# Attention of the first two batches as quads of heads in 64x64 tiles, and the first MLP product of batch 0 in 64x64 tiles at two banks

## The chip, the cores and the metric

The kernel runs on one core of one Trainium2 chip. The metric is the device time of one execution in microseconds. The core has a matrix engine (TensorE, PE in the profile; its weight loads are PEld), VectorE (DVE), ScalarE (ACT), GpSimd (POOL) and SyncE (SP). Each engine takes its own instructions in the order written and waits on semaphores for the others. Matmuls read SBUF and write PSUM, which has eight banks of 128 x 512 float32.

## The reference

Attention with a softmax whose denominator has one more term, then an MLP with a squared ReLU. Batch is 8, heads 12, sequence 448, head size 64; 3584 tokens, model width 768, hidden width 2048.

```python
scores = scale * np.matmul(q, k.transpose(0, 1, 3, 2))
m = np.max(scores, axis=-1, keepdims=True)
e = np.exp(scores - m)
attn = e / (np.sum(e, axis=-1, keepdims=True) + np.exp(-m) + 1e-09)
x = np.matmul(attn, v)
h = x @ w_in
out = (np.maximum(h, 0.0) ** 2) @ w_out
```

Inputs and output are float32; the kernel computes in float16 with float32 sums.

## The kernel before

**Order.** The schedule is written by hand: program order is each engine's order. Every batch passes three stages: scores, exp, sums and values (attention, into `xt`); first MLP product with squared ReLU (into the ring `gs`); second MLP product (into `ot`, then stored). The attention of one batch is interleaved with the MLP of the batch before it, in lists of visits with shares of MLP work between them.

**Batches 2 to 7** take heads in quads: four heads at once, keys in chunks of 64, all products in 64x64 tiles, so that four small products run side by side. `visit` (L317) computes one chunk's scores of four heads into a pair of banks `sp` and its exp; `add_quad` (L350) adds the chunks on DVE; `sums_quad` (L365) multiplies by ones on TensorE and takes the reciprocal with Ln and Exp on ACT; `values_quad` (L381) multiplies with V and normalises. Batch 2's transposes are made by TensorE (`transposes_quad`, L184), later ones by the DMA queue from staged copies.

**Batches 0 and 1** take heads in pairs with keys in chunks of 112 (four neighbouring tokens to a partition). `scores` (L228) has products of 64x112, `values` (L269) of 112x64, `transposes` (L207) of 112x64. Each array shape is another mode of TensorE. `add_chunks` (L247) adds the exps on DVE, `row_sums` (L277) sums over partitions on TensorE and takes the reciprocal, `normalise` (L294) multiplies. Batch 0 is done in two query ranges, of 192 and 256, so that the MLP of the first can run while the second is computed. 18 units (pair, range) follow each other in three loops; `drain` puts pieces of the first MLP product of batch 0 between their steps by shares that were fixed by hand. `keep_warm` (L590) puts filler matmuls between the first transposes.

**MLP.** `product` (L415) runs either as two products of 128x64 or whole. `tile_in` (L435) makes 128 hidden columns for up to 512 tokens in one bank from `mp_tile` (L404), `relu_squared` (L425) evicts it with one ReLU (DVE, or ACT for some) and one square on DVE; `tiles_in_early` (L450) starts before the last heads are there. `tile_out` (L477) makes the second product.

**PSUM.** `sp`: two pairs of banks, for scores. `mp`: three single banks, `xp`: one; from the end of batch 1 `mp_tile` takes turns among the four.

**Loads.** q and k of the first three pairs come as float32 over the SP and ACT queues, all else over POOL's queue, converted to float16: V and the remaining pairs of batch 0, `win` in eight parts, batch 1, then two quads of batch 2 and `wout`. POOL's queue keeps the written order.

Of the kernel before, what the change touches and what calls it, by code (L numbers as in the profile page):

```python
# [16 lines left out]
def kernel(  # L17
# [14 lines left out]
    NPAIR = H // 2  # L32
# [3 lines left out]
    P = S // RUN  # L36
    NQ = H // 4
    KC = S // 64
    PAIRED = (0, 1)
    ON_PE = (0, 1, 2)  # L40
    COLS = H * S // 2 + 16
    HALF = DM // 2

# [19 lines left out]
    m_psum = ctx.enter_context(tc.tile_pool(name="m_psum", bufs=3, space=bass.MemoryType.PSUM))  # L63
# [9 lines left out]
    q_r = q.rearrange("b h (p t) d -> b p h t d", t=RUN)  # L73
    k_r = k.rearrange("b h (p t) d -> b p h t d", t=RUN)
    v_r = v.rearrange("b h (p t) d -> b p h t d", t=RUN)
    win_r = moe_w_in.rearrange("(c p) f -> p c f", p=128)
    wout_r = moe_w_out.rearrange("(c p) f -> p c f", p=128)

    whole, vns, qks, xts, naturals, stages = {}, {}, {}, {}, {}, {}

    def quads_of(t, t0, n, run):

        return t[:, :, t0:t0 + n * run].rearrange("b (i x) (p t) d -> b i p x (t d)", i=2, t=run)

    def load_v_quads(b):
        vn = vns[b] = v_pool.tile([128, NQ, 2, KC, D], FP16, name="vn")
        for i in range(2):
            rows_ = vn[64 * i:64 * i + 64].rearrange("p g j c d -> p (g j) (c d)")
            parts = ((0, KC),) if b in ON_PE else ((0, KC - 1), (KC - 1, KC))
            for c0, c1 in parts:  # L90
                nc.gpsimd.dma_start(out=rows_[:, :, c0 * D:c1 * D], in_=quads_of(v, 64 * c0, 64, c1 - c0)[b, i])

    def load_natural_quads(b, g0, g1):
        t = nat.tile([128, RUN * 2 * S], FP16, name=f"nn{0 if g0 == 0 else 1}")
        w = 2 * S
        for n, r in enumerate((q, k)):
            part = t[:, n * (g1 - g0) * w:(n + 1) * (g1 - g0) * w].rearrange("p (h x) -> p h x", x=S)
            for i in range(2):
                nc.gpsimd.dma_start(out=part[64 * i:64 * i + 64], in_=quads_of(r, 0, 64, KC)[b, i][:, 2 * g0:2 * g1])
            for g in range(g0, g1):  # L100
                naturals["qk"[n], b, "quad", g] = part[:, 2 * (g - g0):2 * (g - g0) + 2].rearrange(
                    "p j (c d) -> p j c d", d=D)

    def load_v(b, p0, p1):
        hs = slice(2 * p0, 2 * p1)
        if b not in vns:
            vns[b] = v_pool.tile([P, H, RUN, D], FP16, name="vn")
        nc.gpsimd.dma_start(out=vns[b][:, hs], in_=v_r[b, :, hs])

    def load_natural(b, p0, p1):  # L110

        raw = b == 0 and p1 <= 3
        for n, r in (("q", q_r), ("k", k_r)):
            src = r[b, :, 2 * p0:2 * p1]
            if raw:
                if p0 == 0:
                    whole[n] = e_pool.tile([P, RUN * S], FP32, name="et")
                t = whole[n][:, p0 * 512:(p0 + 1) * 512].rearrange("p (h t d) -> p h t d", h=2, t=RUN)
                (nc.sync if n == "q" else nc.scalar).dma_start(out=t, in_=src)
            else:  # L120
                if p0 % 3 == 0 and n == "q":
                    whole["both"] = nat.tile([P, RUN * 2 * S], FP16, name=f"nn{p0 // 3}")
                w = NPAIR * RUN * D
                t = whole["both"][:, w * (n == "k"):w * (n == "k") + w].rearrange("p (h t d) -> p h t d", t=RUN, d=D)
                t = t[:, 2 * (p0 % 3):2 * (p0 % 3 + p1 - p0)]
                nc.gpsimd.dma_start(out=t, in_=src)
            for pr in range(p0, p1):
                naturals[n, b, pr] = t[:, 2 * (pr - p0):2 * (pr - p0) + 2]

    def load_win(i, n):  # L130
        w = DF // n
        nc.gpsimd.dma_start(out=win[:, :, i * w:(i + 1) * w], in_=win_r[:, :, i * w:(i + 1) * w])
# [4 lines left out]

# [30 lines left out]

# [13 lines left out]
    def transposes_quad(b, g):  # L184
        if b not in qks:
            qks[b] = qk_pool.tile([128, 3, COLS], FP16, name="qk")
        for n in range(2):
            tp = mp_tile(FP16).rearrange("p a x -> p (a x)")
            for c in range(KC):
                for j in range(2):  # L190
                    nc.tensor.transpose(tp[64 * j:64 * j + 64, 128 * c:128 * c + 128],
                                        naturals["qk"[n], b, "quad", g][:, j, c, :], ident)
            nc.vector.tensor_copy(  # L193
                qks[b][:, n, 2 * S * g:2 * S * (g + 1)].rearrange("p (i c x) -> p c i x", i=2, c=KC),
                tp[:, 0:2 * S].rearrange("p (c i x) -> p c i x", c=KC, i=2))

    def cast(b, pr):
        for name in "qk":
            f = flat.tile([P, 2, RUN, D], FP16, name=f"flat{name}")
            if pr < 2 and name == "k":  # L200
                nc.scalar.activation(out=f, in_=naturals[name, b, pr], func=AF.Copy)
            else:
                nc.vector.tensor_copy(f, naturals[name, b, pr])
            naturals[name, b, pr] = f

    def transposes(b, pr):
        tp = mp_tile(FP16)  # L207
        for i, name in enumerate("qk"):
            for s in range(RUN):
                for h in range(2):  # L210
                    nc.tensor.transpose(tp[64 * h:64 * h + 64, i, P * s:P * s + P],  # L211
                                        naturals[name, b, pr][:, h, s, :], ident[0:P, 0:P])
        if b not in qks:
            qks[b] = qk_pool.tile([128, 3, COLS], FP16, name="qk")
        parts = (0, S // 2, S) if b == 0 and pr < 3 else (0, S)
        for x, y in zip(parts, parts[1:]):
            nc.vector.tensor_copy(qks[b][:, 0:2, pr * S + x:pr * S + y], tp[:, :, x:y])


# [4 lines left out]
    def chunk(et, u, c, kk):  # L224

        n = u[3]
        if n < S:
            return et[:, 0:RUN * 2 * n].rearrange("p (c h j n) -> p c h j n", c=2, h=2, j=2)[:, c, :, kk % 2, :]  # L228
        return et.rearrange("p (k x) -> p k x", k=RUN)[:, kk]

    def scores(u, et, c, only=(0, 1)):
        b, pr, q0, n = u
        qk = qks[b]
        two = [] if n == S else s_psum.tile([P, 2, 512], FP32, name="sp")
        for kk in [2 * c + x for x in only]:
            sp = s_psum.tile([P, 2, 512], FP32, name="sp") if n == S else two
            o = 0 if n == S else kk % 2 * n
            for h in range(2):
                r = slice(64 * h, 64 * h + 64)
                x = pr * S  # L240
                nc.tensor.matmul(sp[:, h, o:o + n], qk[r, 1, x + P * kk:x + P * kk + P],  # L241
                                 qk[r, 0, x + q0:x + q0 + n], start=True, stop=True)
            if n == S:
                exp(chunk(et, u, c, kk).rearrange("p (o x) -> p o x", o=2), sp[:, :, 0:S])
        if n < S:
            exp(et[:, 0:RUN * 2 * n].rearrange("p (c h x) -> p c h x", c=2, h=2)[:, c], two[:, :, 0:2 * n])

    def add_chunks(u, et, es, half, step):
        n = u[3]
        if n == S:  # L250
            e = et.rearrange("p (k x) -> p k x", k=RUN)
            if step < 2:
                nc.vector.tensor_add((es, half[:, 0:2 * S])[step], e[:, 2 * step], e[:, 2 * step + 1])
            else:
                nc.vector.tensor_add(es, es, half[:, 0:2 * S])
        elif step == 1:
            nc.vector.tensor_add(half[:, 0:4 * n], et[:, 0:4 * n], et[:, 4 * n:8 * n])
        elif step == 2:
            f = half[:, 0:4 * n].rearrange("p (h j n) -> p h j n", h=2, j=2)
            nc.vector.tensor_add(es[:, 0:2 * n].rearrange("p (h n) -> p h n", h=2), f[:, :, 0, :], f[:, :, 1, :])  # L260

    def of_head(e, u, h):

        b, _, _, n = u
        if n < S:
            return e[:, h]
        return e.rearrange("p (h x) -> p h x", h=2)[:, h]

    def values(u, et, xp, o=0):  # L269
        b, pr, _, n = u  # L270
        for kk in range(RUN):
            for h in range(2):
                nc.tensor.matmul(xp[64 * h:64 * h + 64, o:o + n], vns[b][:, 2 * pr + h, kk, :],  # L273
                                 of_head(chunk(et, u, kk // 2, kk), u, h), start=(kk == 0), stop=(kk == RUN - 1))

    def row_sums(us, sums):

        n = us[0][3]
        m = n * len(us)
        zp = mp_tile()  # L280
# [573 lines left out]
```

## Time and profile before

| what | us |
|---|---|
| median of 3 runs (lowest to highest) | 407.35 (407.05 to 407.85) |
| span of the profiled execution | 405.9 |
| PE busy, tails of matmuls included | 394.9 (97%) |
| DVE busy | 277.2 (68%) |
| ACT busy | 224.1 (55%) |
| POOL busy | 59.5 (15%) |
| first exp of batch 0 | 7.54 |
| first scores of batch 1 | 36.21 |
| first visit of batch 2 | 68.59 |
| second MLP tile of batch 1 | 83.06 |

A line of the timeline gives start and duration in us, engine, source line, operation, output<-input, the array shape used (64*112 is 64 rows by 112 columns), the operand's partitions x elements, and how many instructions are merged into it; brackets tell how long the engine was idle before and who released it. A row of the stretches gives the stretch, its length, busy us (instructions) of PE, PEld, DVE, ACT, POOL, granted clock of TensorE, DMA share, and GB/s. The waits give engine, tile and line, whom it waited for, total us, times, longest. Matmuls overlap, and their recorded duration holds a tail: the next starts before it ends.

### The profile page before, as it was taken

How to read it: one execution, taken by the hardware profiler on the slowest of the kernel's cores; microseconds unless marked ns; L12 is line 12 of the kernel's file. 1: busy time of each engine (PE TensorE's matmuls, PEld its weight loads, DVE VectorE, ACT ScalarE, POOL GpSimd, SP SyncE). 2: the span in 40 equal slices, each digit the busy share in tenths (PEclk: the TensorE clock that was granted, in tenths of full speed). 3: DMA queues.
4: the chain of work that ended last, by engine and by line, in shares of the span. 5: the costliest groups of instructions: out<-in, count | busy, mean ns of one | idle time of the engine just before them, and what ended most of it. 6: DMA issues, size and time to landing. Idle time of an engine off the chain costs nothing.

```text
span 405.9 us, 14479 instructions
## 1 busy us (share of the span) xinstructions
PE 394.9 (97%) x6627; PEld 262.4 (65%) x6627; DVE 277.2 (68%) x507; ACT 224.1 (55%) x277; POOL 59.5 (15%) x93
## 2 busy tenths in 40 slices
PE   7899998999999999999999999999999999999997
PEld 3567676667676666757666675757666675555664
DVE  3778888786967867686967867686967868186000
ACT  4898986928465564836466473836466473100111
POOL 6524140005000320003200440005000000000000
PEclk9999999999999999999999999999999999999999
DMA  9999999498706794186925694186501020100222
GB/s 186 197 197 198 203 204 208 105 196 113 175 3 126 122 186 102 42 134 144 189 69 129 119 191 95 42 155 122 120 3 40 3 80 4 48 31 0 79 78 79
DMA packets 77118, 45.83 MB, mean 113 GB/s; under 512 B 46720, under 2 KB 71552, under 8 KB 77056
## 3 DMA queue, kind: packets, MB, share of 16 engines
q0 software_dynamic: 30128, 22.16, 36.5%
q1 hardware_dynamic: 46208, 22.05, 24.5%
q8 instruction: 52, 0.85, 0.9%
q10 hardware_dynamic: 720, 0.69, 0.7%
q14 instruction: 10, 0.08, 0.1%
HBM read 45.69 MB, written 17.93 MB: 157 GB/s over the span
## 4 chain that ended last, share of the span: by engine, by line
PE 87%; DVE 5%; ACT 3%; DMA 2%; issue 1%; ACTq 0%; DVEq 0%
PE mp L491 26%; PE mp L419 22%; PE mp L421 10%; PE xp L419 6%; PE mp L390 6%; PE sp L346 5%; PE xp L421 4%; ACT et L222 2%; DMA et<-in_k_dram 2%; PE sp L241 2%; PE xp L273 2%; PE sp L332 1%; PE mp L211 1%; PE xp L491 1%; PE sp L375 1%
## 5 line engine op out<-in xcount | busy, mean ns | idle before, releaser
L222 ACT ACTIVATE et<-sp 128x896 f16<-128x896 f32 (+3 forms) x132 | 118.0, 915 | 26.0 <-PE sp L346 13.0
L491 PE MATMUL mp<-wout,gs 64*64 64x384 f16 x1760 | 125.6, 323 | 0.0
L419 PEld LDWEIGHTS <-win 128*64 128x64 f16 x1536 | 85.0, 110 | 47.7 <-issue 7.2
L419 PE MATMUL mp<-xt,win 128*64 128x448 f16 (+2 forms) x1248 | 109.0, 324 | 2.2 <-DVE qk L193 1.3
L491 PEld LDWEIGHTS <-gs 64*64 64x64 f16 x2624 | 76.2, 107 | 23.0 <-issue 0.6
L491 PE MATMUL xp<-wout,gs 64*64 64x384 f16 x864 | 84.7, 323 | 0.0
L431 DVE TENSOR_SCALAR rt<-mp 128x448 f16<-128x448 f32 (+2 forms) x82 | 51.0, 622 | 19.0 <-PE mp L419 8.4
L433 DVE TENSOR_TENSOR gs<-rt 128x448 f16<-128x448 f16 (+2 forms) x128 | 50.4, 395 | 12.0 <-ACT rt L429 7.9
L222 ACT ACTIVATE nn<-sp 128x896 f16<-128x896 f32 x42 | 37.6, 913 | 14.0 <-PE sp L346 12.3
L429 ACT ACTIVATE rt<-mp 128x448 f16<-128x448 f32 x18 | 9.8, 543 | 60.0 <-PE mp L419 48.3
L498 DVE TENSOR_SCALAR ot<-mp 128x384 f32<-128x384 f32 x41 | 22.7, 554 | 27.3 <-PE xp L491 19.9
L181 POOL COPY flatq<-qk 64x384 f16<-64x384 f16 x20 | 13.6, 704 | 186.9 <-DMA qk<-stage_k 186.6
L421 PEld LDWEIGHTS <-gs 128*128 128x128 f16 x256 | 24.4, 98 | 15.1 <-issue 0.4
L346 PE MATMUL sp<-qk 64*64 64x224 f16 x720 | 32.9, 258 | 0.0
L419 PE MATMUL xp<-xt,win 128*64 128x448 f16 x288 | 31.3, 352 | 0.0
L421 PE MATMUL mp<-wout,gs 128*128 128x384 f16 (+2 forms) x192 | 29.6, 313 | 0.0
L346 PEld LDWEIGHTS <-qk 64*64 64x64 f16 x720 | 22.4, 119 | 10.7 <-issue 3.6
L500 ACT ACTIVATE ot<-mp 128x384 f32<-128x384 f32 (+2 forms) x12 | 5.6, 463 | 42.4 <-PE mp L421 42.4
L396 DVE TENSOR_TENSOR xt<-mp,rcp 128x448 f16<-128x448 f32 x34 | 19.7, 619 | 8.2 <-PE mp L390 7.8
L378 ACT ACTIVATE rcp<-sp,one_b 128x896 f32<-128x896 f32 x18 | 18.1, 1003 | 6.3 <-PE sp L371 6.3
L390 PEld LDWEIGHTS <-vn 64*64 64x64 f16 x504 | 14.4, 107 | 6.1 <-issue 0.4
L390 PE MATMUL mp<-et,vn 64*64 64x448 f16 x308 | 18.3, 349 | 0.0
(82 smaller groups left out, 392.6 us busy)
## 6 DMA issues: line engine op xcount, KB each, us to landing
out_dram<-ot SPq DMA_DIRECT2D x9, 384.0 KB, 2.3
win<-in_moe_w_in_dram POOLq DMA_DIRECT2D x8, 384.0 KB, 14.0
wout<-in_moe_w_out_dram POOLq DMA_DIRECT2D x4, 768.0 KB, 17.8
vn<-in_v_dram POOLq DMA_DIRECT2D x10, 288.0 KB, 5.4
out_dram<-ot SPq DMA_DIRECT2D x15, 192.0 KB, 3.0
stage_q<-in_q_dram POOLq DMA_DIRECT2D x4, 676.0 KB, 9.8
stage_k<-in_k_dram POOLq DMA_DIRECT2D x4, 676.0 KB, 12.3
out_dram<-ot SPq DMA_DIRECT2D x7, 288.0 KB, 6.0
```

The costliest lines, as they stand in the source:

```text
L181: nc.gpsimd.tensor_copy(km[rows_].rearrange("p h (x o) -> p h x o", o=2)[:, :, :, odd], src[:, :, S // 2 - 32:S // 2])
L222: nc.scalar.activation(out=out_, in_=in_, func=AF.Exp, scale=scale)
L346: nc.tensor.matmul(sp[64 * i:64 * i + 64, o, j * n:(j + 1) * n], keys, qk[r, 0, h * n:(h + 1) * n], start=True, stop=True)
L378: nc.scalar.activation(out=rcp, in_=zp[:, :, 0:S], func=AF.Ln, bias=one_b)
L390: nc.tensor.matmul(xps[i][64 * j:64 * j + 64, 0:S], vns[b][r, g, j, c, :], of_column(e[r], m, j), start=(c == 0), stop=(c == KC - 1))
L396: nc.vector.tensor_mul(xts[b][:, NQ * i + g, :], xps[i][:, 0:S], zqs[m][:, i, :])
L419: nc.tensor.matmul(out_[x:x + 64], lhsT[:, x:x + 64], rhs, start=start, stop=stop)
L421: nc.tensor.matmul(out_, lhsT, rhs, start=start, stop=stop)
L431: nc.vector.tensor_scalar(out=rt[:, 0:m], in0=hp[:, 0:m], scalar1=0.0, scalar2=None, op0=ALU.max)
L433: nc.vector.tensor_mul(gs[:, f0:f0 + per, t0 % RING:t0 % RING + n], r, r)
L491: nc.tensor.matmul(o[y:y + 64, 0:w], g[x:x + 64, y:y + 64], wout[x:x + 64, fb, n0:n0 + w], start=(fb == 0), stop=(fb == NFFB - 1))
L498: nc.vector.tensor_scalar(out=ot[:, n0:n0 + w], in0=op[:, 0:w], scalar1=OUT_SCALE, scalar2=None, op0=ALU.mult)
```

## The change

Batches 0 and 1 use quads too. The pairs' code goes (`scores`, `values`, `transposes`, `add_chunks`, `row_sums`, `normalise`, the three loops, `drain`, `tiles_in_early`, the fillers after the first nine). Batch 1 becomes quads with `visit`, whole query range. Batch 0 becomes quads in two query halves of 224; its sums are made by TensorE, by multiplying every exp chunk with ones beside the values. Its first MLP product is made by `Square` in blocks of 512 hidden columns by 224 tokens: 96 products of 64x64 in a pair of banks, the upper rows writing one bank while the lower rows write the other, then the other way round. Between the two turns a SyncE no-op that waits for the first and releases the second keeps them apart. One ReLU and one square evict 896 columns at once.

Heads are paired anew (heads 2g, 2g+1, 6+2g, 7+2g are a quad), with `win`'s rows laid out to match, in all batches. `mp` and `xp` become one pair of banks each; `mp_pair` and `mp_tile` take turns among the pairs. The two values' banks of a quad are normalised by one multiply instead of two. q and k of the first quad come as float32, in two halves; `win` comes in four parts of two loads each; loads are by quad. The values and the sums of batch 1's last quad fall into batch 2's first visits, where before those of its last pair did.

Core of the new code (all matmuls go through `mm`):

```diff
+    def half_scores(at):
+        g, half, k = HALVES[at]
...
+        for x in range(len(two[0])):
+            for o in range(2):
+                if x < len(two[o]):
+                    c, j = two[o][x]
+                    r = slice(64 * j, 64 * j + 64)
+                    for i in range(2):
+                        s0 = (2 * g + i) * S
+                        mm(sp[64 * i:64 * i + 64, o, x * FIRST:(x + 1) * FIRST], qk[r, 1, s0 + 64 * c:s0 + 64 * c + 64],
+                           qk[r, 0, s0 + q0:s0 + q0 + FIRST], start=True, stop=True)
...
+    def half_post(at):
...
+        if (g, half) not in xzs:
+            xzs[g, half] = pair_of("xp")
+        xz, e = xzs[g, half], half_e(g, half)
+        todo = [p for x in zip(*pieces(at)) for p in x]
+        for is_sum in range(2):
+            for c, j in todo:
+                for i in range(2):
+                    r = slice(64 * i, 64 * i + 64)
+                    key = (g, half, i, j)
+                    mm(xz[64 * j:64 * j + 64, i, is_sum * FIRST:(is_sum + 1) * FIRST],
+                       ones[r] if is_sum else vns[0][r, j, g, c, :], e[r, j, c], start=key not in opened,
+                       stop=bool(is_sum) and c == KC - 1)
...
+    def half_finish(g, half):
...
+        nc.scalar.activation(out=rcp, in_=xz[:, :, FIRST:2 * FIRST], func=AF.Ln, bias=one_b)
+        nc.scalar.activation(out=rcp, in_=rcp, func=AF.Exp, scale=-1.0)
...
+        nc.vector.tensor_mul(xts[0][:, 2 * g:2 * g + 2, q0:q0 + FIRST], xz[:, :, 0:FIRST], rcp)
...
+    def posts(*ats):
+        for at in ats:
+            half_post(at)
+            if HALVES[at][2] == 3:
+                half_finish(*HALVES[at][0:2])
...
+    class Square:
...
+        def part(self, flip, dcs=range(DCH)):
...
+            for jf in range(2):
                 for dc in dcs:
+                    self.done += 1
+                    for o in range(2):
+                        r = (o + flip) % 2
+                        rows_ = slice(64 * r, 64 * r + 64)
+                        for y in (0, 64):
+                            f = (self.f0 + 2 * o + jf) * 128 + y
+                            got = mm(hp[y:y + 64, o, jf * n:(jf + 1) * n], win[rows_, dc, f:f + 64],
+                                     xt[rows_, dc, x0:x0 + n], start=self.done == 1, stop=self.done == total,
+                                     bank=(self.t0, self.f0, o, y), row=r)
+                            if self.last:
+                                after(got, self.last)
+                                self.last = None
+            if self.done < total:
+                self.last = nc.sync.nop()
+                after(self.last, got)
+            if self.done == total:
+                relu_squared(hp[:, :, 0:2 * n], self.t0, n, self.f0, 4, self.act)
...
+    in0 = [Square(0, 4 * x) for x in range(4)]
+    in1 = [Square(FIRST, 4 * x) for x in range(4)]
+    early, late = range(2 * NQ - 2), range(2 * NQ - 2, 2 * NQ)
+    pre = {
+        12: [lambda: in0[0].part(0, early)],
+        15: [lambda: in0[0].part(0, late)],
+        16: [lambda: in0[1].part(0)],
+        17: [lambda: in0[1].part(1)],
+        19: [lambda: in0[2].part(0)],
+        20: [lambda: in0[2].part(1)],
+        22: [lambda: transposes_quad(1, 0, "mp")],
+    }
+    behind = {
+        3: [lambda: transposes_quad(0, 1, "mp")],
+        7: [lambda: transposes_quad(0, 2, "mp")],
+        12: [lambda: in0[0].part(1, early)],
+        14: [lambda: in0[0].part(1, late)],
+    }
+    done = {at: (at - 2,) for at in range(2, 24)}
+    done[12], done[13] = (10, 11), ()
+    for at in range(24):
+        if at > 1:
+            half_scores(at)
+        for f in pre.get(at, ()):
+            f()
+        posts(*done.get(at, ()))
+        if at > 1:
+            half_exp(at)
+        for f in behind.get(at, ()):
+            f()
...
+    plan = {
+        0: [lambda: posts(22)],
+        1: [lambda: in0[3].part(0), lambda: posts(23)],
+        2: [lambda: in0[3].part(1)],
+        3: [lambda: transposes_quad(1, 1, "mp")],
+        5: [lambda: in1[0].part(0)],
+        6: [lambda: in1[0].part(1)],
+        8: [lambda: in1[1].part(0)],
+        9: [lambda: in1[1].part(1), lambda: sums_quad(0, False), lambda: values_of(0, 2)],
+        10: [lambda: values_of(0, 5)],
+        11: [lambda: transposes_quad(1, 2, "mp")],
+        13: [lambda: in1[2].part(0)],
+        14: [lambda: in1[2].part(1)],
+        16: [lambda: in1[3].part(0), lambda: sums_quad(1, False), lambda: values_of(1, 2)],
+        17: [lambda: in1[3].part(1), lambda: values_of(1, 5)],
+        19: [lambda: transposes_quad(2, 0, "mp")],
+        20: [lambda: transposes_quad(2, 1, "xp")],
+    }
```

`HALVES` counts the 24 steps of batch 0: half 0 of quads 0, 1, 2, then half 1, four steps each; `after(a, b)` makes a wait for b. `FIRST` is 224. In `pre` work stands behind a step's scores and ahead of the posts of the step two before; `behind` stands after the step's exp. A group is the four steps of a quad and half, 0 to 3, 4 to 7 and so on; the fourth has one chunk instead of two.

## The prediction

> **What bounds the kernel now.** I read the page first (span, chain), then the busy time by stretch, the waits of the opening, and the timeline at the joints. The run itself is 405.9 us of span; the median of the runs shown is 407.35, so 1.45 us lie around it, and I add them at the end.
>
> ```profile
> span 405.9 us, 14479 instructions
> ...
> PE 87%; DVE 5%; ACT 3%; DMA 2%; issue 1%; ACTq 0%; DVEq 0%
> ```
>
> The chain that ended last is TensorE for 87%. From batch 2 on there is little else: a batch takes 46 us there (its first MLP tile starts at 126.1, 172.3, 218.1 in the chain), and the change alters neither number, shape nor order of its matmuls. What it rebuilds lies before the first visit of batch 2, at 68.59. The stretches (us of busy time of PE, PEld, DVE, ACT, POOL; clock; DMA):
>
> ```profile
> 5.40:36.20 30.80, 28.03 (x476) 19.43 (x476) 22.57 (x50) 26.59 (x36) 12.61 (x17) 1.00 1.43 201
> 36.20:68.60 32.40, 30.16 (x481) 22.04 (x479) 27.75 (x53) 27.38 (x37) 9.52 (x14) 1.00 1.31 204
> 68.60:82.00 13.40, 12.75 (x285) 8.73 (x285) 9.41 (x15) 12.49 (x15) 0.00 (x0) 1.00 0.62 132
> ```
>
> In the opening 63.2 us no engine is full: ACT 54.0, DVE 50.3. PE's 58.2 holds the tails of matmuls, so I count its stream by start distances:
>
> ```profile
> 54.51 1.37 PE L419 MATMUL mp<-xt,win 128*64 128x256 f16 x22
> ...
> 55.80 0.58 PE L241 MATMUL sp<-qk 64*112 64x448 f16 x4
> ...
> 56.24 1.72 ACT L222 ACTIVATE et<-sp 112x896 f16<-112x896 f32 x2
> ...
> 56.32 0.97 PE L191 MATMUL mp<-ident,nn 128*64 128x128 f16 x28
> ```
>
> Eleven pairs of 256 columns at 0.109 make 1.20; the next shape starts after 1.29: a change of array shape costs 0.09. The two exps take 1.72 where one takes 0.92: the next may start after 0.80. Batches 0 and 1 alternate three shapes: I count 72 changes up to 68.6. In batch 2 and later all is 64x64:
>
> ```profile
> 121.52 0.36 PE L346 MATMUL sp<-qk 64*64 64x224 f16 x8
> 121.71 0.97 PE L491 MATMUL mp<-wout,gs 64*64 64x384 f16 x17
> ```
>
> Eight 64x64 products of 224 columns hold the array for 0.19, 24 ns each. Who waited for whom from 5.4 to 68.6:
>
> ```profile
> ACT et L222 <- PE sp L241: 6.4, 11, 2.2
> DVE rt L431 <- PE mp L419: 4.4, 4, 1.4
> ```
>
> **The loads, edit by edit.** TensorE before: MLP 192 pairs (0.0825 and 0.109) 18.4, scores 9.1, values 8.4, sums 2.1, transposes 6.3, warm-up fillers 1.3 = 45.6, and 72 changes at 0.093 = 6.7: 52.3. After, at 24 ns per 224 columns: 8 MLP blocks of 96, 18.4; scores of batch 0 4.4 and of batch 1 4.0; values and sums of batch 0 4.0 each and 0.8 because the first two steps use one half of the rows; values of two quads 2.65, two sums 0.4; transposes 7.3 (seven quads' 28 in 0.82 by L191, and 28 of the first quad at 0.056, as they fill one half of the columns): 46.0, and 20 changes, 1.9: **47.9**. So the quads give back in switching what TensorE pays for the sums.
> ACT before: 24 exps at 0.80, 12 at 0.91, 12 at 0.70, 11 Ln/Exp pairs 13.4, casts 1.3 = 53. After: 39 at 0.81, 6 at 0.43 (L429, 448 elements, 0.54 less the overlap), 6 Ln/Exp at 1.24, 2 at 1.95 (L378, L379), casts 1.2: **46.7**. DVE loses all adds of batch 0 (12.1 by L257, L260): about **42** of 50.3.
> By loads alone all fall. What decides is how long TensorE, which takes its work in written order, stands idle: now 63.2-52.3 = 10.9.
>
> **The new waits, walked.** Every engine keeps the written order. Prices: an exp may start 0.40 after its scores start (0.44 at 68.59/69.03) and blocks the scores two steps on, as `sp` has two buffers; posts (values and sums of a step) 0.38; a quad's transposes 0.82, and its scores can start 1.75 after they began (last matmul's tail 0.22, copy 0.62, hand-overs); half an MLP block 1.15. Not in the trace: ReLU of 128x896, between 0.62 (L431 at 448) and 1.25 (two of them); 384, 448 and 512 elements take 0.552, 0.622, 0.686, so 1.09, and the one `mp` pair is free 1.4 after the block's last matmul. One `xp` pair holds values and sums of a group: the next group's posts can start only after Ln 0.64, Exp 0.58 and the multiply 0.62, so 1.95 after Ln.
>
> ```
>  7.5  exp 0, as now (7.54): same 224 KB, same casts
> 14.3  scores 4: first copies end 10.5 (exp 2 at 10.95), posts 0, 1 at 0.77
>       each, quad 1's transposes 12.5; ACT idle 12.3-14.7
> 20.2  scores 8: quad 2's transposes 18.45; ACT idle 18.7-20.6
> 26.1  Ln of group 2: behind an MLP piece and two posts; ACT idle 1.5
> 34.9  Ln of group 3: late MLP piece ends 30.1 (one turn at the banks shows,
>       0.4), ReLU frees mp 31.5, block half to 32.65, posts 33.05, scores,
>       block half 34.4, posts 34.6; ACT idle 31.7-34.9
> 37.1  posts 16 wait for its multiply; TensorE idle 34.8-37.1
> 41.6  Ln of group 4; posts 20 wait to 43.55 (idle 1.05)
> 44.7  first visit of batch 1 (now 36.2)
> 50.1  transposes: Ln 47.1, multiply 49.0, ReLU 50.1; idle 48.4-50.1
> 55.9  third block: ReLU behind two adds; idle 54.85-55.9
> 66.7  last block: ReLU 65.55-66.65; idle 1.05
> 73.4  first visit of batch 2 (now 68.59)
> ```
>
> Batch 0's 37 us hold some 24 of TensorE work; batch 1's 28.7 hold 23, about what it takes now (32.4 with more MLP in it). TensorE idle 68.0-47.9 = 20.1, **+4.8** at the joint.
>
> Then batch 2's first visits: 48 steps of second product 7.8, 12 scores 2.3, two sums 0.4, and now the values of a whole quad 1.3 = 11.8; the sum of quad 2 waits 0.75 for its last add (last exp ends 73.7, add 0.65), Ln/Exp 1.95 delays the exps and the third to fifth visits wait 0.85: end 86.85, transposes 87.8, second MLP tile 89.0. Now:
>
> ```profile
> 81.60 1.65 PE L419 MATMUL mp<-xt,win 128*64 128x448 f16 x12 [0.64 <-ACT rcp L290]
> 83.06 1.33 PE L419 MATMUL xp<-xt,win 128*64 128x448 f16 x12
> ```
>
> 89.0-83.06 = **+5.9**, of it 1.1 here: the wait for the last pair's reciprocal (0.64 and more inside the 1.65) goes, the longer Ln/Exp comes.
>
> Costed at nothing, with cover. Transfers: at 198 GB/s the first quarter of `win` is in by 20 (used from 24.5), batch 1's quads by 30, 39 and 42 (used 41.6, 50.1, 60.4); batch 2's loads and `wout` now start behind the transposes at 42.5 and end by 63, used after 75; were it not so, a 4 us piece would show. PSUM in pairs of banks from batch 2 on: a pair waits for two evictions, but ReLU and square take 1.02 (L431, L433) against 1.13 of a tile, and the multiply of a quad comes once: between -0.3 and +0.5 in all, I take 0. Turns through SyncE: ten; nine have 0.57 or more of other work before the next piece. The nearest row for SyncE is its 0.4 per issue, so each could show 0 to 0.4: 0 to +3.6, I take 0.4, as SP has nothing else queued there.
>
> The clock: 1.00 in all stretches above, with fillers between the first transposes. The change drops those. [...] No row here shows a halved clock.
> [...]
>
> **Rivals.**
> 1. Faster. The place is the 20.1 us of idle TensorE: in the walk 6.7 of it are posts that wait for a group's Ln, Exp and multiply, 5 are ReLUs on `mp`, and I may have put these too long or one behind the other where they overlap. If idle stays at the 10.9 of now, the joint comes at 5.4+47.9+10.9 = 64.2, -4.4, and with the 1.1 behind it -3.3: **404.0**. The lower loads of ACT and DVE speak for it, the written order against. It decides where idle falls below 63.2-47.9-1.1 = 14.2.
> 2. The opening runs on a slow clock: up to 24 us it streams some 10 us. Were the clock a half there, these would take 20; with some two thirds of the 10 hidden in the idle time of the walk, +3 on my sum: **416**. The unbroken 1.00 of now speaks against it.
> 3. It doesn't do what it says: the turns don't hide, +3.2 on my sum: **416.5**. 64x64 products at two banks run four abreast now (L491, L346), which speaks against.
> 4. Waits move and the sums cancel: 407.3.
>
> **The numbers.** 405.9+5.9+1.45 = **413.2**; by the bounds (walk +-2, turns, pairs) the likeliest case reaches 410 to 416. Chances: forecast 0.60, rival 1 0.23, rivals 2 and 3 0.12 together, rival 4 0.05. A range of 402.5 to 417.5 takes these in and leaves 2 in 10. Measurement can tell about 0.2%. Faster 0.23, same 0.05, slower 0.72.
>
> **To be seen after.** First visit of batch 2 near 73 and second MLP tile of batch 1 near 89; ACT gaps of 2 to 3 us at 12, 19 and 32; `xp` posts waiting for DVE's multiply; 24 ns per 224-column product; the same 46 us per batch behind. I am wrong if the joint comes before 68, or if a batch behind it takes another time.

## The result and the profile after

498.59 us, median of 4 runs (495.83 to 501.3), against 407.48 (407.05 to 407.85): ratio 1.2225, 95% interval 1.2177 to 1.2274. Slower, as forecast, but by 91 us where I had 6; the range ended at 417.5. The profiled execution took 499.0 us, its span 497.2.

The page of the changed kernel: span, granted clock in 40 slices, chain.

```profile
span 497.2 us, 15787 instructions
...
PEclk8897988699999999999999999999999999999999
...
PE 75%; DVE 16%; ACT 5%; issue 3%
```

TensorE carried 87% of the chain and DVE 5%; now DVE carries 16%, and the clock is no longer full in the first fifth. The joints (us; the stream is the time in which TensorE's products follow each other, idle is the rest; both are counted from start distances, as in the prediction):

| stretch | before | predicted | after | miss |
|---|---|---|---|---|
| first visit of batch 2 at | 68.59 | 73.4 | 94.78 | +21.4 |
| of it TensorE idle from 5.4 on | 10.9 | 20.1 | 34.5 | +14.4 |
| of it TensorE stream | 52.3 | 47.9 | 54.9 | +7.0 |
| from there to the second MLP tile of batch 1 | 14.5 | 15.6 | 19.4 | +3.8 |
| from there to the end of the span | 322.8 | 322.8 | 383.0 | +60.2 |

Seven tenths of the miss lie where I had put nothing. The stretches of after (busy us and instructions of PE, PEld, DVE, ACT, POOL; clock; DMA share; GB/s):

```profile
5.40:54.80 49.40, 32.14 (x876) 27.18 (x877) 14.94 (x26) 24.25 (x35) 11.96 (x18) 0.86 0.85 138
54.80:94.78 39.98, 29.52 (x774) 23.60 (x766) 24.52 (x31) 23.56 (x28) 9.20 (x13) 0.86 1.05 168
94.78:114.17 19.39, 16.65 (x314) 11.92 (x313) 10.65 (x17) 13.78 (x15) 0.00 (x0) 0.86 0.28 60
114.17:497.20 383.03, 330.88 (x5376) 222.37 (x5375) 214.45 (x361) 155.98 (x189) 32.09 (x52) 1.00 0.39 78
```

In the last row the clock is full, the DMA share is down to 0.39, and no engine is busy for more than 331 of 383 us: what is left are waits. Whom TensorE waited for (total us, times, longest):

```profile
PE mp L109 <- DVE rt L454: 19.9, 25, 1.7
...
PE xp L109 <- DVE rt L454: 15.6, 16, 1.5
...
PE mp L219 <- DVE qk L221: 9.8, 7, 2.5
...
PE xp L109 <- ACT rt L452: 7.6, 12, 0.6
```

L454 and L452 are the ReLUs of the MLP tiles, L221 the copies behind a quad's transposes. The timeline of after at the first MLP tiles of batch 1:

```profile
113.50 0.63 DVE L454 TENSOR_SCALAR rt<-xp 128x448 f16<-128x448 f32 x1 [0.51 <-PE xp L109]
114.16 0.39 DVE L456 TENSOR_TENSOR gs<-rt 128x448 f16<-128x448 f16 x1
114.17 1.33 PE L109 MATMUL xp<-xt,win 128*64 128x448 f16 x12 [0.72 <-DVE rt L454]
...
115.31 1.33 PE L109 MATMUL mp<-xt,win 128*64 128x448 f16 x12
...
116.51 1.08 DVE L387 TENSOR_TENSOR half<-et 128x1792 f16<-128x1792 f16 x1
117.51 0.62 DVE L454 TENSOR_SCALAR rt<-mp 128x448 f16<-128x448 f32 x1
...
118.18 1.33 PE L109 MATMUL mp<-xt,win 128*64 128x448 f16 x12 [1.54 <-DVE rt L454]
```

The second tile in `xp` (114.17) starts when the ReLU of the first tile in `xp` ends (113.50 + 0.63), though the two have different banks. The third, in the other pair, follows at once; the fourth, again a second half, waits 1.54, as its ReLU stands behind an add of 1.08. So the wait comes at every second tile. `mp_tile` hands out the two halves of one tile, and in these lines the write to one half starts only when the reader of the other half, ahead of it in program order, has ended. By start distances TensorE is idle for 61.8 us from 114 on, 54 of them ended by these ReLUs, 5.8 by the evictions at L542; before had 1.9.

The same in the opening: `transposes_quad` puts q and k into one tile and copies q in between.

```profile
14.97 0.58 PE L219 MATMUL mp<-ident,nn 128*64 128x128 f16 x14
15.59 0.62 DVE L221 COPY qk<-mp 128x896 f16<-128x896 f16 x1 [3.81 <-PE mp L219]
16.27 0.58 PE L219 MATMUL mp<-ident,nn 128*64 128x128 f16 x14 [0.72 <-DVE qk L221]
...
16.89 0.62 DVE L221 COPY qk<-mp 128x896 f16<-128x896 f16 x1 [0.67 <-PE mp L219]
...
17.57 0.39 PE L109 MATMUL sp<-qk 64*64 64x224 f16 x8 [0.72 <-DVE qk L221]
```

### The profile page after: what moved, and what is told of

It reads as the page before. It is cut to its first block, busy times and chain, and to the rows that moved or that the text cites. A ratio compares the mean times of both kernels' runs of the same rounds, so it can differ in the third digit from the quotient of the medians.

```text
span 497.2 us, 15787 instructions
## 1 busy us (share of the span) xinstructions
PE 413.4 (83%) x7341; PEld 286.7 (58%) x7341; DVE 265.7 (53%) x441; ACT 219.4 (44%) x268; POOL 57.9 (12%) x93
## 4 chain that ended last, share of the span: by engine, by line
PE 75%; DVE 16%; ACT 5%; issue 3%
PE xp L109 33%; PE mp L109 32%; PE sp L109 8%; DVE rt L454 7%; DVE half L387 2%; ACT rt L452 2%; DVE qk L221 1%; PE mp L219 1%; DVE half L389 1%; DVE ot L539 1%; DVE ot L538 1%; ACT ot L542 1%; DVE xt L424 1%; DVE xt L325 1%; DVE gs L456 1%
## 5 line engine op out<-in xcount | busy, mean ns | idle before, releaser
L109 PEld LDWEIGHTS <-win 128*64 128x64 f16 (+2 forms) x2016 | 108.8, 114 | 105.5 <-issue 69.5
L251 ACT ACTIVATE et<-sp 128x896 f16<-128x896 f32 (+1 forms) x129 | 113.9, 898 | 56.8 <-PE sp L109 52.9
L109 PEld LDWEIGHTS <-gs 64*64 64x64 f16 (+1 forms) x2880 | 103.2, 107 | 42.1 <-issue 6.8
L109 PE MATMUL mp<-xt,win 64*64 64x224 f16 (+2 forms) x1392 | 100.7, 317 | 26.6 <-DVE rt L454 19.2
L109 PE MATMUL xp<-wout,gs 64*64 64x384 f16 (+1 forms) x1920 | 110.5, 324 | 2.3 <-ACT ot L542 2.3
L109 PE MATMUL xp<-xt,win 128*64 128x448 f16 (+1 forms) x624 | 74.1, 353 | 23.2 <-DVE rt L454 15.6
L454 DVE TENSOR_SCALAR rt<-mp 128x448 f16<-128x448 f32 (+1 forms) x58 | 39.9, 688 | 60.0 <-PE mp L109 58.9
L109 PE MATMUL sp<-qk 64*64 64x224 f16 (+1 forms) x1056 | 61.6, 284 | 6.1 <-ACT et L251 1.7
L109 PE MATMUL mp<-wout,gs 64*64 64x384 f16 (+3 forms) x960 | 60.3, 320 | 2.3 <-ACT ot L542 1.6
L456 DVE TENSOR_TENSOR gs<-rt 128x448 f16<-128x448 f16 (+1 forms) x120 | 49.7, 414 | 21.3 <-ACT rt L452 17.3
L452 ACT ACTIVATE rt<-xp 128x448 f16<-128x448 f32 x18 | 9.8, 543 | 77.8 <-PE xp L109 77.8
L454 DVE TENSOR_SCALAR rt<-xp 128x448 f16<-128x448 f32 x38 | 23.7, 624 | 22.4 <-PE xp L109 21.7
L542 ACT ACTIVATE ot<-mp 128x384 f32<-128x384 f32 (+2 forms) x8 | 3.6, 450 | 42.4 <-PE mp L109 42.4
```

The source lines that it names most:

```text
L109: return nc.tensor.matmul(out_, lhsT, rhs, start=start, stop=stop)
L251: nc.scalar.activation(out=out_, in_=in_, func=AF.Exp, scale=scale)
L452: nc.scalar.activation(out=r, in_=hp, func=AF.Relu)
L454: nc.vector.tensor_scalar(out=r, in0=hp, scalar1=0.0, scalar2=None, op0=ALU.max)
L456: nc.vector.tensor_mul(gs[:, f0:f0 + per, t0 % RING:t0 % RING + n], r, r)
L542: nc.scalar.activation(out=ot[:, n0:n0 + w], in_=op[:, 0:w], func=AF.Copy, scale=OUT_SCALE)
```

## The experiments

Theory A: the waits for the other half's ReLU make the 60 us. Theory C: the wait for q's copy makes part of the opening's loss. Theory D: the slow clock makes part of it. Theory F, formed after the first runs: in idle times that nothing in the profile ends, TensorE waits for instructions. Theories E and G: waits that are left in the opening, E for the one pair of banks for values and sums, G for copies one behind the other.

**Theory A, from both sides.** `own_pair` takes the sharing away, `before_wait` adds the wait alone to the kernel before.

```diff
 # own_pair, in mp_tile
-        if not spare:
-            t = mp_pair()
-            spare.extend([t[:, 0], t[:, 1]])
-        return spare.pop(0)
+        return mp_pair()[:, 0]
 # before_wait, in tile_in of the kernel before (product hangs it on its first matmul)
+        if joined[0] >= 0 and f0 % 2:
+            wait_for[0] = relu[0]
```

> The changed kernel, but every MLP tile takes a pair of banks for itself and uses one bank of it, so that its first matmul no longer waits for the ReLU of the tile before. Theory A (the two halves of a pair are one tile, and the second half's matmuls wait for the ReLU of the first): from the second MLP tile of batch 1 to the end 383 us become 325 to 335, as the TensorE idle time of 49 + 13 us ended by L454, L452 and L542 goes and only two banks in turn instead of four are left; the whole 498.6 becomes 440 to 452. Rival (two pairs instead of four banks: a tile waits because too few buffers are free, or DVE is late anyway): half as many buffers leave it at 490 or more.

> The kernel before with one thing added: from batch 1 on the first matmul of every second MLP tile waits for the ReLU of the tile ahead of it, though the two tiles have banks of their own. The computation is the same. Theory A: 56 such waits (8 a batch, 7 batches) of the matmul's tail 0.2, the ReLU 0.55 to 0.62 and two hand-overs, 0.8 to 1.1 each, longer where an add of 1.1 stands ahead on DVE: 407.5 becomes 452 to 472. Rival (the pairing costs because a pair is free only when both its halves are evicted, not by this wait): at most 415.

Measured: own_pair 442.95 (440.86 to 444.85; 1.0849 of before, 1.0805 to 1.0893), 55.6 us less than the changed kernel; before_wait 466.56 (465.47 to 467.47; 1.1428, 1.1399 to 1.1456), 58.6 more than the kernel before. In before_wait:

```profile
PEld L419 <- DVE rt L443: 41.2, 30, 2.0
...
PEld L419 <- ACT rt L441: 19.2, 18, 1.1
```

By start distances 40.6 us end with DVE's ReLU in 38 places and 14.4 with ACT's in 18; in after 39.6 in 38 and 14.4 in 18. Theory A holds: the same waits, put into the old kernel, cost what they cost in the new one, and its rival (at most 415) falls.

**Are pairs as such harmless?** `pairs_last` (on `both`, below) uses both halves again, with both products ahead of both ReLUs.

```diff
+        if f0 % 2 == 0:
+            halves[0] = mp_pair()
+        hp = halves[0][:, f0 % 2]
...
+        if f0 % 2:
+            for f in (f0 - 1, f0):
+                relu_squared(halves[0][:, f % 2, 0:n], t0, n, f, 1, f in relus_on_act[0])
```

> The kernel `both`, but the two halves of a pair are used again by two MLP tiles: both products first, then both ReLUs and squares, so that all four banks serve. Theory A says that the pairing as such is harmless and only the order of the second product behind the first ReLU costs: no slower than both (437.5), and up to 3.5 us less, as that is the idle time left at L452 between 100 and 360 us: 434 to 437. Rival (a pair is evicted as a whole and so comes free late): slower than both by 5 us or more.

Measured 436.67 (435.86 to 438.8), `both` 437.54 (436.36 to 438.13): no slower, the ranges overlap. It is the order of the second product behind the first ReLU that costs, not the pairing.

**Theory C.** `copies_last` emits all 28 transposes ahead of the copies; `both` joins it with own_pair.

```diff
                                         naturals[which, b, g][:, j, c, :], ident)
-            nc.vector.tensor_copy(quad_columns(b, n, g, slice(0, 128)),
+        for n in range(2):
+            nc.vector.tensor_copy(quad_columns(b, n, g, slice(0, 128)),
```

> The changed kernel, but a quad's 28 transposes of q and k all come ahead of the two copies, so that k's transposes no longer wait for the copy of q. Theory C (this wait costs the opening TensorE time, 13.4 us over ten quads, and the idle time then halves the clock): where no product of the same quad follows at once (quads 1 and 2 of batch 1, the first two of batch 2) 0.9 to 2.7 us go each, and some of the stretches at clock 0.50 behind them; first visit of batch 2 at 83 to 89 instead of 94.8, the whole 484 to 492. Rival (the idle time only moves, because the scores then wait for the same two copies): first visit of batch 2 at 92 or later, the whole 495 or more. The steady state behind must not change.

> Both edits, MLP tiles in pairs of their own and the copies behind all transposes. If the two causes are separate, the gains add: by theories A and C 428 to 442. If the first gain is taken back by the second (one clock, one DVE), it is no lower than own_pair alone by 4 us. By neither theory does it come under the 407.5 of the kernel before, since the opening stays longer than before's.

Measured 492.6 (490.7 to 493.04): 6 us less, just short of the 484 to 492 that I expected; the first visit of batch 2 came at 87.45, within the 83 to 89. `both` took 437.54, 5.4 less than own_pair, so the gains add. In copies_last:

```profile
15.45 1.36 PE L219 MATMUL mp<-ident,nn 128*64 128x128 f16 x28
...
16.86 1.15 DVE L222 COPY qk<-mp 128x896 f16<-128x896 f16 x2 [4.59 <-PE mp L219]
...
18.07 0.39 PE L109 MATMUL sp<-qk 64*64 64x224 f16 x8 [1.25 <-DVE qk L222]
```

From transposes to scores it is 2.62 here (the transposes mostly at half clock) and 2.60 in after. One quad later, with the clock full in both kernels, it is 2.2 (22.25 to 24.48) against 2.60: where the scores follow at once, 0.4 goes and the rest of the wait moves, as the rival said. Still, the idle time that these copies end falls from 13.4 us in after to 5.8. In `both` the first visit of batch 2 stands at 86.84.

**Theory D, the clock.** `before_cold` takes the fillers out of the kernel before (the first nine stay), `warm` puts nine into the first two idle times of `both`.

```diff
 # before_cold
-    keep_warm(1)
...
-            keep_warm(1)
...
-        if i in (1, 3, 5):
-            keep_warm(1 + i // 5)
 # warm
+    keep_warm(5)
     first_casts(raw, 1)
...
     first_transposes(1, 0, 4, "xp")
+    keep_warm(4, "mp")
```

> The kernel before without the fillers between its first transposes (the first nine stay), which is the one part of the change that touches them. Theory D (the idle time there halves the clock): the clock shows 0.5 for some 3 to 7 us behind 8 us, and the time is 1 to 3 us longer, 409 to 411. Rival (the fillers do nothing: the order of transposes and casts sets the pace): the clock is 1.00 and the time 407 to 408.2.

> The kernel `both` with nine fillers of 128x512 in the two first idle times of TensorE (1.13 and 0.86 us before the first two groups of scores), as before had fillers there. Theory D (idle time there lets the clock fall to 0.50 from 9 to 15.6 us, and that costs): the clock is 1.00 up to 16 us, TensorE's 5.8 busy us there shrink by up to 2.9, and 1 to 2.5 us of it reach the first visit of batch 2: 435 to 436.5. Rival (the opening waits for copies and exps there, and the clock costs nothing): the clock is 1.00 and the time the same as both, 437 to 438.

before_cold: 412.71 (410.39 to 414.25; ratio 1.0106, 1.0073 to 1.0139), 4.6 us longer, more than I expected, and clear of the rival's 407 to 408.2. The same stretch in before_cold, then in before:

```profile
11.00:28.40 17.40, 16.46 (x188) 11.90 (x184) 9.17 (x20) 12.19 (x18) 8.37 (x11) 0.51 1.45 197
```

```profile
11.00:28.40 17.40, 15.81 (x263) 10.97 (x261) 12.51 (x27) 16.19 (x23) 8.59 (x11) 1.00 1.45 197
```

In the same 17.4 us TensorE, busy for 16.46 and 15.81 of them, gets through 188 matmuls at clock 0.51 and 263 at 1.00. In this execution the exps are 0.1 us early at 12 us, 4.3 late at 29, and 4.0 late at the first exp of batch 2: the lag grows in the slow stretch (11.20 to 28.26) and nowhere else. So D fits the profiled execution. For the kernel as such it is not shown: of the six executions two show a mean granted clock of 1.00, and they took 414.25 and 413.88, the longest of all. Why these two are slow without the fillers is open, as they left no trace.

`warm`, however, took 437.03 (436.35 to 437.67), no gain: the clock is full up to 39.4, the exp of step 4 comes at 15.73 instead of 18.26 and that of step 16 at 32.88 instead of 35.25, but the first exp of batch 2 only at 86.71 instead of 87.27. In between, gaps that no one ended grew from 3.4 to 6.9 us, and the clock fell from 39.4 to 46.2 and from 87.2 to 94.0: the fillers moved the slow stretches more than they removed them (13.7 us up to 94 here, 17.1 in `both`).

**Theory F, instructions.** Such a gap, in `both`, in the middle of a block of 48 products:

```profile
37.54 0.87 PE L106 MATMUL mp<-xt,win 64*64 64x224 f16 x26
40.45 0.76 PE L106 MATMUL mp<-xt,win 64*64 64x224 f16 x22 [2.04 <-issue]
```

"issue" means that the profile knows of no releaser. I listed the gaps of over 0.3 us of this kind in all traces; some of the 30, with the number of weight loads and matmuls ahead of each, the remainder of that number by 256, and the landing of the last 16 KB packet on the DMA queue that the page lists as `q8 instruction` (57 packets, 0.93 MB in after) (us):

```
kernel       resumes   gap   instructions ahead  rest by 256   packet landed
after          35.10  1.15          958              190           33.68
after          41.02  1.93         1214              190           39.69
both           40.45  2.21         1214              190           38.98
copies_last    62.85  0.78         2238              190           61.48
warm           85.06  1.88         3262              190           83.70
before_wait   165.26  1.18         5050              186           163.76
```

All 25 in kernels built from after stand at rest 190, all 5 in those built from before at 186, and each ends 1.2 to 1.6 us after a packet. `whole_rows` makes batch 0's first MLP product of half as many products, of 128 rows by 64 columns, one bank after the other; `rows_turns` puts the turns through SyncE back into that; `rows_warm` puts the fillers into it.

```diff
 # whole_rows, Square.part(o, dcs)
+                    for y in (0, 64):
+                        f = (self.f0 + 2 * o + jf) * 128 + y
+                        mm(hp[y:y + 64, o, jf * n:(jf + 1) * n], win[:, dc, f:f + 64], xt[:, dc, x0:x0 + n],
+                           start=self.done[o] == 1, stop=self.done[o] == 2 * DCH)
 # rows_turns, behind a part that is not the last
+                self.last = nc.sync.nop()
+                after(self.last, got)
```

> The kernel `both`, but the first MLP product of batch 0 is made of products of 128 rows by 64 columns, one bank after the other, without turns and without SyncE's no-ops. The stream is as long by the rows of before (two abreast instead of four), and some 30 changes of array shape come back at 0.093 each. If the turns at two banks cost nothing, as I said: 438 to 441. If the turns show (my third rival): 433 to 436.5.

> The kernel whole_rows with the ten turns put back: the second part of each block waits, through a no-op on SyncE, for the first part, as in the changed kernel. It tells the turns from the number of instructions. If the turns cost (my third rival), 3 us or more come back: 436.5 to 438. If they hide and theory F holds (half the instructions is what whole_rows gained): 433.5 to 434.8.

> The kernel whole_rows with the nine fillers of warm. In warm the fillers brought the scores 4 to 16 of batch 0 forward by 2.4 us, and the gain was gone at the end of batch 1, where idle times of TensorE that nothing in the profile ended had grown from 3.4 to 6.9 us. Theory F (these are TensorE waiting for instructions: each ends 1.2 to 1.5 us after a packet of 16 KB on an instruction queue, and stands at instruction 190 of every 256; whole_rows has half the MLP instructions and none of them): here the gain of the clock stays, 433.9 becomes 431 to 432. Rival (ACT's or DVE's order behind step 16 sets the joint whatever the clock was): 433.5 to 434.5.

whole_rows: 433.87 (432.99 to 438.85), 3.7 less than `both` in the median, and in the range that I had given to turns that show (433 to 436.5). One run lies above all of `both`; its granted clock is 0.968, that of the others 0.983 to 0.988. The profile has none of these gaps. rows_turns, which tells the turns from the number of instructions: 435.27 (434.08 to 436.37), between its two forecasts, and again no such gap: 1.4 for ten turns, not resolved from nothing, and below the 3 us of my third rival.

rows_warm: 434.28 (432.68 to 435.48): no gain, F's forecast of 431 to 432 missed. Its trace says little about F, because the lead was hardly there: the fillers stood in front of the first scores, the first exp came at 8.34 instead of 7.10 in whole_rows, and the exp of step 4 at 16.49 instead of 16.78. This lead of 0.3 us stayed: the first exp of batch 2 comes at 82.41 instead of 82.69, the span is 430.9 instead of 431.2. What the traces show is where these gaps stand, the packet 1.2 to 1.6 us before each ends, and their absence in all four kernels with half the instructions in that product; that TensorE ran short of instructions in them is my reading, as the profile names no releaser, and that they ate the gain of `warm` is not shown.

**What is left of the opening.** `later_posts` issues the first values and sums of a group one step later; `k_on_act` joins whole_rows, pairs_last and the fillers and copies k on ACT beside q on DVE.

```diff
 # later_posts
+    for at in (6, 10, 18, 22):
+        done[at], done[at + 1] = (), (at - 2, at - 1)
 # k_on_act
+            if n:
+                nc.scalar.activation(out=quad_columns(b, n, g, slice(0, 128)), in_=src, func=AF.Copy)
+            else:
+                nc.vector.tensor_copy(quad_columns(b, n, g, slice(0, 128)), src)
```

> The kernel `both`, but the first values and sums of a group (steps 4, 8, 16, 20) are issued one step later, behind the scores of the next step, so that the Ln, Exp and multiply of the group before have 0.8 us more. Theory E (the one pair for values and sums makes TensorE, and behind it the scores, wait: 1.4, 1.4, 2.0 and 0.8 us in both): 2 to 4 us go, 433.5 to 435.5. Rival (ACT sets the pace there, and what TensorE no longer waits it waits for the exp): within 1 us of 437.5.

> The best parts together: whole_rows, fillers, both halves of a pair used with the ReLUs last, and the copy of k of every quad on ACT beside the copy of q on DVE. Theory G (what is left of the loss up to the first visit of batch 2 is idle TensorE behind serial copies, 6.4 us in whole_rows): 0.6 us goes for each of seven quads less what ACT pays, 427 to 430. Rival (ACT is as late as DVE there, so a copy of 0.75 on it delays the exps): 431 or more. By neither does it come below the 408 of before.

later_posts: 439.83 (438.65 to 442.41), 2.3 slower, where the rival had within 1 us of `both`. The wait passed on to the exps, as the rival said: in `both` TensorE waits 5.4 us for the multiply (L323) and 2.4 for exps, in later_posts 7.9 for exps and so little for the multiply that it is not listed:

```profile
PE sp L106 <- ACT et L249: 7.9, 9, 2.0
```

k_on_act: 436.08 (431.7 to 436.72), no gain, within the rival's 431 or more. The copies did not run side by side:

```profile
L221 ACT ACTIVATE qk<-mp x7: 917/917/917, 14.7 to 105.8; 128x896 f16<-128x896 f16 x7
...
  DVE qk L223: 9.1, 7
```

ACT's copy takes 0.917 (DVE's 0.618), and before 7 of the 8 ACT stood idle, 9.1 us in all, until DVE's copy ended. Both write the one tile `qk`, so this fits theory A; it was not tried with separate tiles. Theory E falls; G's gain did not come, but since the copies stayed one behind the other, its premise was not put to the test.

No run came below the kernel before.

## Why the prediction was wrong

**The failed step** is "PSUM in pairs of banks from batch 2 on: a pair waits for two evictions ... between -0.3 and +0.5 in all, I take 0", and with it "the change alters neither number, shape nor order of its matmuls". I asked when a pair comes free for its next user, and not what stands between its two halves. Own_pair gives 55.6 us for it, before_wait 58.6, so both show this wait and not the number of buffers. The second sign of being wrong came true: a batch takes 54 us instead of 46. Number and shapes of the matmuls had stayed (5376 from the second MLP tile of batch 1 on, in both kernels), and, but for one place in a later batch, their order; what had changed was which ones share a tile. That the change is slower was forecast for the opening alone, so that most of the 91 us have another cause than the one that I gave.

**Transposes, "0.82, and its scores can start 1.75 after they began".** 2.60 in after. I counted one copy of 0.62 where q and k need two, one behind the other, and missed that k's transposes wait for the first. The wait costs 6 us (copies_last); with it gone the start still comes after 2.2 at full clock, so some 0.5 a quad was mis-sized in any case.

**The clock.** My sum has no time for a slow clock: I took the 1.00 of before to stay, though the fillers went. That failed, and rival 2's premise (the opening on a slow clock) came true, in more places than it had. In after the records show 0.50 from 8.16 to 14.99, 42.30 to 49.12, 62.78 to 66.19, 76.43 to 79.84 and 90.08 to 100.32, though the longest idle time of TensorE that the timeline lists up to there is 2.54 us. What precedes each fall is a stretch of 3.41 us in which TensorE was busy for 26 to 58%. A half block of 48 products takes 2.40 with the clock at 0.50 (62.67) and 1.34 at full clock (68.22). Up to 94.78 these are 25 us at half clock, and in 19 of them TensorE streams, so up to 9.6 us of stream are the price, by an estimate from the 19 and the 0.50. The stream rose by 7.0 over my 47.9, so that I had it some 2.6 too long at full clock. Of the 3.8 behind the joint it is up to 2.8 (5.5 us at half clock). This is read from traces. Runs of one kernel point the same way (rows_warm: 432.68 and 433.08 at a mean clock of 0.991 and 0.988, 435.48 twice at 0.980), but no experiment held the clock full up to the joint, and before_cold is slower at full clock too.

**Idle in the walk, 20.1.** 34.5 in after. Without theories A and C, in `both`, 28.9, and in whole_rows 24.4 up to 82.26. Of the 28.9, by who ended it: copies 6.1, the one pair for values and sums 6.1 (I had 6.7), ReLUs 4.8 (I had 5), exps 3.3, nothing that the profile shows 3.4, the first quad's copies 3.6. So the walk's order was right where it had a wait, and it had none for these 3.4 and too little for copies, which also hold `mp` against the next MLP block (0.91 and 1.38 in `both`).

**Right.** 24 ns per 224-column product, a half block 1.15, the ReLU of 896 columns 1.09, first exp (7.35 against 7.5); the ten turns cost 1.4 us in the medians, not resolved from nothing (I took 0.4); slower rather than faster: rival 1 asked for less idle, and it rose.

**What remains open.** With the waits of A and C shortened and the gaps of F absent, whole_rows has a span of 431.2 where my sum has 411.8, so 19.4 are left: 8.9 at the first visit of batch 2 (82.26 against 73.4), 3.5 up to the second MLP tile (19.15 against 15.6), where the clock is 0.91, and 7.0 behind it (329.8 against 322.8), where the MLP tiles turn between two banks instead of four. pairs_last, with four, has 327.7 there, so 2 of the 7 go with the banks; the rest was not tried singly. Of the 3.5, more than 2 lie in a term that I had mis-sized: "the sum of quad 2 waits 0.75 for its last add". In `both` and in whole_rows TensorE waits 2.9 us there, once; in `both`:

```profile
PE sp L106 <- DVE half L391: 2.9, 1, 2.9
```

In whole_rows this add (84.85) stands on DVE behind two adds and two pairs of copies of the transposes, which the walk left out.

## What to carry to other kernels

When buffers are merged, ask for every pair of users what the second waits for in program order: here a tile was waited for as a whole, and a reader emitted between two writers to its halves stopped the second one. Emit all writers first, then all readers, or keep separate tiles; and look for it in stages that the change seems to leave alone, because a wait of 1 us at every second tile is worth more there (55.6 us here) than all of a reordered opening. Count every copy on the way from a transposed tile to its user, and read the granted clock of the new kernel stretch by stretch: in after it was 0.50 behind stretches of 3.41 us with TensorE busy for 26 to 58%, though the timeline lists no idle time over 2.54 us up to the last of these falls.

## What the runs showed of the hardware

In these traces the granted clock was 1.00 or 0.50, and the slow stretches lasted whole multiples of 3.41 us: in after 3.41 (from 62.78), 6.83 (from 8.16) and 10.24 (from 90.08), in before_cold 17.07 (from 11.20). In after a fall came behind a stretch of 3.41 us in which TensorE was busy for 26 to 58%; stretches of 51 to 58% without a fall occur too (18.4 to 28.6 us), so no threshold is shown.

TensorE stopped for 0.4 to 2.2 us, with no releaser in the profile, always 190 instructions past a multiple of 256 in kernels built from after and 186 in those built from before, and went on 1.2 to 1.6 us after 16 KB had arrived on the queue `q8 instruction`. In after and in `both` such gaps stood in the blocks of 64x64 products of 24 ns with one weight load each (35.10 and 41.02, 40.45); in whole_rows, with the same MLP product in half as many products, none showed.
